# Eight turns of an attention and gated-layer kernel in one written order, one copy moved to ScalarE, and W2's last results re-ordered

## The chip, the cores and the metric

One Trainium2 chip, one of its cores. The metric is the device time of one execution in microseconds (us). The kernel before took 838.37 us, the median of three runs (838.03 to 839.97).

## What is computed

Float64 weights and float32 activations come in; the output is float32. 3072 tokens of width 512 go through three layers:

```python
# 1. chunked attention, 8 heads of 64, queries in chunks of 32, 56 keys + 8 memory keys each
a = softmax(q_c @ k_full.T / 8);  x = a @ v_full
# 2. 512 -> 1024 -> 512
h = x @ w_in;  e = exp(h - max(h));  solu = h * e / (sum(e) + 1e-9)
ln = (solu - mean) / sqrt(var + 1e-6) * g_ln;  x2 = ln @ w_out
# 3. 512 -> 2048 -> 512
g = x2 @ w_in2;  out = max(0.01 * g, g) @ w_out2
```

All large products are split into a high and a low half (three 128x512 matmuls for one product of 128 rows), so that TensorE computes them at its full rate and the result keeps float32 accuracy. The float64 weights are decoded on the chip: an Abs on ScalarE, four VectorE operations on the raw words, then the halves.

## The kernel before, in words

**Tiles.** The tokens form 24 tiles of 128. A tile goes through these steps; the names are those of the profile.

- Attention of tile a: `s_scores` (32 small matmuls into `att`, L213, then a maximum on VectorE, L222 and L223), `s_exp` (eight exponentials on ScalarE, L230), `s_rs` (L237, L238), `s_pt` (four transposes into `tr`, L243, and a copy of the result to `pt` on VectorE, L248), `s_pv` (32 small matmuls, L264, and a scaling on VectorE, L270), `x_halves` (four transposes, L282, the high half on ScalarE, L286, the low half on VectorE, L288).
- First product: `h_steps`, 24 matmuls of 512 columns into `h` or into the tile `spare`, whose name in the profile is `x2p` (L299).
- The norm, `norm_steps`: maximum (VectorE, L315), exponential (ScalarE, L319), product and sum (VectorE, L321 to L328), square (ScalarE, L331), variance (VectorE, L333) and its power -0.5 (GpSimd, L335), and the final scaling, either on GpSimd (L338, L339, for the tiles in `ON_POOL`) or on VectorE (L341).
- Transposed halves of the result, `s_lt`: through TensorE in two groups of four transposes (L351, L353, L354), or, for the tiles in `BOUNCE`, through VectorE's transposes of 32x32 blocks and DRAM (`lt_steps`: L365, stored by L371, read back by L376, L389, L387).
- Second product, `s_o`: one of the four output chunks of a block of four tiles at a time, 24 matmuls of 512 columns into `x2p` (L401), then a copy on ScalarE and a store (`put_x2`, L409, L410). The program calls such a chunk a W2 result; there are 24.

**Stages.** (1) The startup decodes W1 and computes tiles 0 to 2 of the attention and the first product of tiles 0 and 1; its order is written out by hand in the string `STEPS`, one character for one step of a named stream. (2) Turns 0 to 7, a loop over `range(STEADY)`: turn i does the attention of tile i+2, the first product and the norm of tile i, the transposed halves of tile i-1, decodes some of the eight slices of W2 (`W2_AT`, `load_w2`: L114 to L129, L137, L138, and the low half on GpSimd, L140), and turn 7 also computes the first three W2 results (`O_AT`). This stage is issued in the order of the loop and each engine's order is then chosen by the compiler's planner. (3) Turns 8 to 24, the function `steady`, again in the written order on all engines (`manual_schedule`): one tile of attention, one tile's first product and one W2 result in each turn, five behind (`LAG`), and one slice of W3 decoded. Turn 24 has no tile left: it computes W2 result 19, the transposed halves of tile 23 and the last piece of W3. (4) The last four W2 results, 20 to 23, run while the third layer's operands are prepared (`x_steps`, L690 to L709; `w3_steps`, L725). (5) The third layer, in a scheme of seven products of half-size blocks (L841 and below).

**Queues.** Nearly all transfers are issued on the queue of the SP engine, in the order of issue: the queries (`load_q`), the keys (`kbd`) and values (`vbd`) of the next tile, the raw slices of W2 and W3 (`raw`). Keys and values have one buffer each, so their loads wait for the matmuls that read the tile before. `x2s`, the tile of `put_x2`, has one buffer; ScalarE issues its store, and in turn 24 also the two stores of the last W3 pair (L508, L509) and, for tile 6, the four reads of L376.

Of the kernel before, what the change touches and what calls it, by code (L numbers as in the profile page):

```python
# [33 lines left out]
ON_POOL = range(6)  # L34

SPARE_PSUM = (1, 3, 5)
# [8 lines left out]
def tile_kernel(  # L45
# [99 lines left out]
    def decode(raw, dh, dl, pool, gain=None, sub=nc.gpsimd):  # L145
        for _ in decode_steps(raw, dh, dl, gain, pool, sub):
            pass
        return lows[-1]


# [48 lines left out]
    def load_tile(i):  # L199
        return *load_qk(i), load_kv(i, vbd, vw)  # L200

    def load_w2(kk):
        decode(
            load_raw(w2[kk * P : (kk + 1) * P, :], dec), w2h[:, kk], w2l[:, kk],
            dec, g_sb[:, kk : kk + 1],
        )

    def s_scores(i, q, k):
        sc = ps_att.tile([P, 8, 64], F32, name="att")
        for hp in range(4):  # L210
            for c in range(4):
                cs = slice(32 * c, 32 * c + 32)
                nc.tensor.matmul(  # L213
                    sc[cs, 2 * hp : 2 * hp + 2, :], q[:, hp, cs], k[:, :, hp, c, :],
                    start=True, stop=True,
                )
        if i % TPB == 0:
            nc.vector.memset(sc[0:32, :, 8:24], NEG)
# [5 lines left out]
        return sc, nms  # L224
# [15 lines left out]
    def pt_steps(p):  # L240
# [7 lines left out]
        nc.vector.tensor_copy(pt, ptp)  # L248
# [6 lines left out]

    def s_pt(p):
        return last(pt_steps(p))
# [17 lines left out]
    def s_pv(pt, v, rs):  # L275
        return last(pv_steps(pt, v, rs))

# [13 lines left out]
    def x_halves(x):  # L291
        return last(xt_steps(x))

# [10 lines left out]

    def s_h(x, h=None, early=False):
        if x is not None:
            if h is None:
                h = ps_h.tile([P, DFF], F32, name="h")
            for _ in h_steps(*x, h):
                pass  # L310
        return last(norm_steps(h, early))
# [32 lines left out]
    def s_lt(so, b, t, lh, ll):  # L344
        ts_ = slice(t * P, (t + 1) * P)
        if TB * b + t not in BOUNCE:
            for g in range(2):
                tp = ps_tr.tile([P, 4, P], F32, name="tr")
                for kk in range(4):
                    f = (4 * g + kk) * P  # L350
                    nc.tensor.transpose(tp[:, kk], so[:, f : f + P], ident)  # L351
                cs = slice(4 * g, 4 * g + 4)
                nc.scalar.activation(lh[:, cs, ts_], tp, AF.Copy)  # L353
                nc.vector.tensor_tensor(  # L354
                    out=ll[:, cs, ts_], in0=tp, in1=lh[:, cs, ts_].bitcast(F32), op=ALU.subtract
                )
            return
        for _ in lt_steps(so, b, t, lh, ll, nc.scalar):
            pass

    def lt_steps(so, b, t, lh, ll, eng):
# [7 lines left out]
        yield  # L369
# [5 lines left out]
        for q in range(4):  # L375
            eng.dma_start(  # L376
# [17 lines left out]
    def s_o(b, ec, lh, ll, part, s=None):  # L394
        if part == 0:
# [3 lines left out]
        for kk in range(4 * part, 4 * part + 4):  # L399
# [5 lines left out]
        if part == 1 and s != 0:  # L405
            put_x2(b, ec, lp.tile([P, BT], F32, name="x2s", bufs=1) if s is None else s)
# [5 lines left out]
    def att_steps(i, ld):  # L412
# [5 lines left out]
        pt = s_pt(p)  # L418
        yield
        x = s_pv(pt, ld[2], rs)  # L420
# [15 lines left out]
    startup = ExitStack()  # L436
    startup.enter_context(
# [48 lines left out]
    startup.close()  # L486
    del xs[:2]
    ld = load_tile(3)
    sst.close()
    lp = sh.enter_context(tc.tile_pool(name="lp", bufs=2, reuse_waits="tile"))  # L490
    lb = {}
    w3m = []
    so = None

    def store_w3(f, m, eng=nc.sync):
# [12 lines left out]
        eng.dma_start(out=w3f[f // 2, :, 2:4], in_=a)  # L508
        eng.dma_start(out=w3f[f // 2, :, 4:7], in_=s)  # L509
# [7 lines left out]
    def leftover(o):  # L517

        o.so = next(o.norm)
        put_x2(*o.x2, lp.tile([P, BT], F32, name="x2s", bufs=1))  # L520
# [6 lines left out]
    def steady(i, o):  # L527
# [4 lines left out]
        def w2(j):  # L532
            s_o(j // TB, j % TB, *lb[j // TB], 0)
            s_o(j // TB, j % TB, *lb[j // TB], 1, 0)
            u.x2 = j // TB, j % TB
# [5 lines left out]
        else:  # L541
            w2(i - LAG)
            store_w3(f - 1, lows[-1], nc.scalar)
# [3 lines left out]
        if i - 1 in BOUNCE:  # L547
            u.lt = lt_steps(o.so, *to, nc.sync)
            next(u.lt)
# [35 lines left out]
        w2(i - LAG)  # L585
        for _ in w3d:
            pass
        next(u.norm)
# [11 lines left out]
    for i in range(STEADY):  # L600
        a = i + 2
        b, t = divmod(i, TB)
        if t == 0:
            lhl = lp.tile([P, 2, KF, BT], F32R, name="lhl")
            lb[b] = (lhl[:, 0], lhl[:, 1])
        att = a > 2
        if att:
            p, rs = s_exp(*s_scores(a, ld[0], ld[1]))
            s_rs(rs)
        if i == max(SPARE_PSUM) + 1:  # L610
            sx2.close()
            ps_x2 = sx2.enter_context(tc.tile_pool(name="ps_x2b", bufs=2, space=PSUM, side="right", reuse_waits="tile"))
        if i < 2:
            nso = s_h(None, hs[i], True)
        else:
# [544 lines left out]
```

## Time and profile before

| | |
|---|---|
| median of three runs | 838.37 us |
| the profiled execution: its own time | 840.38 us |
| the profiled execution: its span, first to last instruction | 838.4 us |
| mean granted TensorE clock | 0.998 of full |
| startup, to the last matmul of tiles 0 and 1 | 0 to 38.6 us |
| turns 0 to 7, to the start of turn 8 | about 38.6 to 130.7 us |
| turns 8 to 24 | about 130.7 to 353 us |
| the last W2 results | about 353 to 377.3 us |
| third layer | 377.3 to 838.4 us |

The profile gives for each engine the time in which it was busy; a matmul's end is modelled, so a row of back-to-back matmuls of 0.39 us each that start every 0.23 us counts as busy throughout. "PEld" is TensorE's loading of weights, "granted clock" the share of TensorE's full clock, of which there are two levels (1.2 and 2.4 GHz); a stretch with a share between has some of each.

### The profile page before, as it was taken

Reading aid. Unit: us, or ns where it says so; the run is one execution under the profiler, and the core shown is the slowest. Engines: PE = TensorE matmul, PEld = TensorE weight load, DVE = VectorE, ACT = ScalarE, POOL = GpSimd, SP = SyncE. Lnnn points to the kernel's source line nnn. Section 1 sums busy time; section 2 is a strip of 40 time slices with the busy share of each in tenths; the row PEclk is TensorE's granted clock in tenths of the full one; section 3 lists DMA queues with packets and bytes.
Section 4 is the critical chain, followed back from the end, with each engine's and each line's share of the span. In section 5 each row is a group of like instructions: output and inputs, shape, how many; then the busy total and the mean of one; then the engine's idle time right before and its main releaser. Section 6 shows DMA issues by size and latency. Waiting matters only on the chain.

```text
span 838.4 us, 13730 instructions
## 1 busy us (share of the span) xinstructions
PE 816.3 (97%) x5014; PEld 666.2 (79%) x5014; DVE 649.7 (77%) x1145; ACT 472.9 (56%) x1067; POOL 54.9 (7%) x63
## 2 busy tenths in 40 slices
PE   6889999999999999999999999999999999999998
PEld 5566778888888888778888888888888888888886
DVE  8989865888888888698888855675699687768663
ACT  5478844555546553457655656677658344544541
POOL 3333300000000000000000000000000000010001
PEclk9999999999999999999999999999999999999999
DMA  9555554888879785833898964586696375546542
GB/s 337 192 165 188 164 189 129 270 261 258 263 252 272 257 247 187 295 127 107 289 339 325 342 233 197 198 325 258 247 382 225 121 255 194 196 164 220 192 147 101
DMA packets 69891, 190.96 MB, mean 228 GB/s; under 512 B 8000, under 2 KB 32064, under 8 KB 65856
## 3 DMA queue, kind: packets, MB, share of 16 engines
q1 hardware_dynamic: 65360, 182.61, 63.4%
q10 hardware_dynamic: 4464, 7.47, 2.4%
q8 instruction: 40, 0.66, 0.3%
q14 instruction: 27, 0.22, 0.1%
HBM read 129.24 MB, written 60.82 MB: 227 GB/s over the span
## 4 chain that ended last, share of the span: by engine, by line
PE 86%; DVE 6%; ACT 4%; POOL 1%; DMA 1%; issue 1%; ACTq 0%; DVEq 0%; POOLq 0%
PE C L841 27%; PE B L841 16%; PE x2p L401 13%; PE A L841 12%; PE h L299 12%; PE att L264 2%; PE att L213 2%; PE tr L282 1%; PE tr L243 1%; ACT p L230 1%; POOL w2l L140 1%; PE x2p L299 1%; DMA kbd<-in_kw 1%; DVE hnm L315 1%; ACT e L331 1%
## 5 line engine op out<-in xcount | busy, mean ns | idle before, releaser
L401 PE MATMUL x2p<-lhl,w2h 128*128 128x512 f32 x384 | 121.2, 396 | 2.0 <-ACT xP L409 1.6
L841 PE MATMUL C<-xP,L 128*128 128x512 f32 x384 | 95.2, 389 | 0.0
L401 PEld LDWEIGHTS x2p<-lhl,w2h 128*128 128x128 f32 x384 | 70.6, 188 | 19.9 <-issue 3.0
L841 PEld LDWEIGHTS C<-xP,L 128*128 128x128 f32 x384 | 72.1, 188 | 15.0
L401 PE MATMUL x2p<-lhl,w2l 128*128 128x512 f32 x192 | 75.1, 391 | 0.0
L299 PE MATMUL h<-w1h,xh 128*128 128x512 f32 x168 | 68.9, 410 | 0.0
L299 PE MATMUL h<-w1h,xl 128*128 128x512 f32 x168 | 66.7, 397 | 1.6 <-DVE xl L288 1.6
L841 PE MATMUL C<-h,L 128*128 128x512 f32 x192 | 66.9, 389 | 0.0
L299 PE MATMUL h<-w1l,xh 128*128 128x512 f32 x168 | 66.4, 395 | 0.0
L949 DVE TENSOR_TENSOR ring<-ring,h 128x512 fp32r<-128x512 f32 x96 | 61.8, 685 | 3.3 <-ACT h L948 2.7
L230 ACT ACTIVATE p<-att,nms 128x64 f32<-128x64 f32 x192 | 57.4, 335 | 6.5 <-DVE nms L223 6.1
L948 ACT ACTIVATE h<-ring 128x512 fp32r<-128x512 f32 x72 | 39.8, 621 | 31.8 <-DMA ring<-gd 19.3
L864 ACT ACTIVATE g<-g 128x512 f32<-128x512 f32 x72 | 45.2, 627 | 21.9 <-DVE g L883 19.0
L319 ACT ACTIVATE e<-h,hnm 128x1024 f32<-128x1024 f32 x21 | 23.5, 1121 | 57.1 <-DVE hnm L315 57.1
L841 PE MATMUL B<-xP,L 128*128 128x512 f32 x192 | 48.9, 390 | 0.0
L948 ACT ACTIVATE h<-t2k 128x512 fp32r<-128x512 f32 x48 | 28.6, 628 | 31.5 <-DVE t2k L941 17.1
L883 DVE TENSOR_TENSOR g<-B,u 128x512 f32<-128x512 f32 x23 | 15.9, 690 | 36.0 <-PE B L841 35.9
L230 ACT ACTIVATION_READ_ACCUMULATOR p<-att,nms 128x1 f32 x192 | 42.7, 222 | 0.0
L401 PEld LDWEIGHTS x2p<-lhl,w2l 128*128 128x128 f32 x192 | 36.1, 188 | 7.6
L841 PEld LDWEIGHTS B<-xP,L 128*128 128x128 f32 x192 | 36.0, 188 | 7.7 <-DVE g L893 0.3
L841 PEld LDWEIGHTS C<-h,L 128*128 128x128 f32 x192 | 36.0, 188 | 7.5
L299 PEld LDWEIGHTS h<-w1h,xl 128*128 128x128 f32 x168 | 31.8, 190 | 9.4 <-DVE xl L288 2.7
(187 smaller groups left out, 1913.0 us busy)
## 6 DMA issues: line engine op xcount, KB each, us to landing
ring<-gd SPq DMA_DIRECT2D x48, 768.0 KB, 4.0
gd<-g SPq DMA_DIRECT2D x24, 1024.0 KB, 4.9
raw<-in_w SPq DMA_DIRECT2D x32, 512.0 KB, 5.8
L<-w3f SPq DMA_DIRECT2D x14, 896.0 KB, 5.7
kbd<-in_kw SPq DMA_DIRECT2D x46, 256.0 KB, 4.4
vbd<-in_vw SPq DMA_DIRECT2D x46, 256.0 KB, 3.8
lnd<-sl SPq DMA_DIRECT2D x16, 512.0 KB, 4.5
xtq<-in_w SPq DMA_DIRECT2D x16, 512.0 KB, 6.3
```

The costliest lines, as they stand in the source:

```text
L140: sub.tensor_tensor(out=dl, in0=m, in1=dh.bitcast(F32), op=ALU.subtract)
L213: nc.tensor.matmul(sc[cs, 2 * hp : 2 * hp + 2, :], q[:, hp, cs], k[:, :, hp, c, :], start=True, stop=True,)
L230: nc.scalar.activation(p[:, h // 2, :, h % 2], sc[:, h], AF.Exp, bias=nms[:, h : h + 1], scale=SCALE, accum_out=rs[:, h : h + 1],)
L264: nc.tensor.matmul(xp[cs, 2 * hp : 2 * hp + 2, :], pt[:, hp, cs], v[:, :, hp, c, :], start=True, stop=True,)
L299: nc.tensor.matmul(h[:, hf * 512 : hf * 512 + 512], a[:, kk], b, start=kk == 0 and j == 0, stop=kk == KD - 1 and j == 2,)
L319: nc.scalar.activation(e, h, AF.Exp, bias=nm, accum_out=rs)
L401: nc.tensor.matmul(ps, a[:, kk, es], r[:, kk], start=(kk == 0 and n == 0), stop=(kk == KF - 1 and n == 2),)
L841: nc.tensor.matmul(acc, w[i], x[j], start=first and n == 0, stop=last and n == 2, skip_group_check=True)
L864: nc.scalar.activation(u.g[:, i], u.g[:, i] if src is None else src, AF.Prelu, alpha=0.01)
L883: tt(out=o.g[:, 1], in0=o.acc["B"], in1=o.u2, op=ALU.add)
L948: nc.scalar.activation(h[:, i], src[n_], AF.Copy)
L949: tt(out=l[:, i], in0=src[n_], in1=h[:, i].bitcast(F32), op=ALU.subtract)
```

## The change

- **One order for turns 0 to 7.** The planner's stage goes. The work of turns 0 to 7 becomes streams of steps: `a` to `h` for the attention of tiles 3 to 10, `0` to `7` for the norms, `i` to `p` for the slices of W2, `A` to `F` for the first products of tiles 2 to 7, `G` to `R` for the transposed halves of tiles 0 to 5 (two groups each), `S` for those of tile 6, `T`, `U`, `V` for W2 results 0 to 2. The last nine steps of `STEPS` join them as `w`, `x`, `y` and `z`. The string `TURNS` of 303 characters gives the order, the same for all five engines.
- **The copy of the transposed probabilities** of tiles 3 to 10 is made by ScalarE (`PT_DVE` is empty).
- **The final scaling of tile 7** goes to GpSimd (`ON_POOL`), from VectorE; tile 6 keeps VectorE.
- **Tile 6's reads from DRAM** (L376) are issued by SP, and no more by ScalarE.
- **Turn 23**: one step of the norm is called between the steps of the decode. **Turn 24**: W2 result 19 is cut into two halves of 12 matmuls, with the transposed halves of tile 23 between them; the norm's last step and `put_x2` come ahead of the last W3 pair's VectorE work and stores.
- **Last W2 results**: five instead of seven steps of `x_steps` come ahead of result 20 and its copy, three more follow that copy.

```diff
-    "zb4155243AAbA5bc4AB766c456B7ABc6B55776B67cABc7ABABc"
+    "zb4155243AAbA5bc4AB766c456B7ABc6B55776B67c"
-W2_AT = {1: (0,), 2: (1,), 3: (2, 3), 6: (4, 5), 7: (6, 7)}
+TURNS = (
+    "iaaiwxxaxi0zy0yizaaa0ybajbiAj0AAAi1bA0A1abAbbj0a1aca1cbGGABcBbbBb2GBjcBbkdk2dcHBjB1j2BcckH"
+    "CC1HcCdle3d23cdcld2CCeckCCIe2J3JC4IdfIk34DJDDdkeeldd3DefDDKfdlLDD3eg4KKLmM4lMLmfefE55EmEME"
+    "lmfEEnNme5n54EgnEmTNNTngeUUTUU45fh6oOe6PTnUoTO56nOFoo66FFppopPpPT6fFFFSFUggQpoUTgpFTUSgRQ7"
+    "QTfV7RhhUVfRV7VhV7VVVgfg7S7hgSgVh"
+)
+PT_DVE = ()
-O_AT = {7: (0, 1, 2)}
-ON_POOL = range(6)
+ON_POOL = (0, 1, 2, 3, 4, 5, 7)
...
-        nc.vector.tensor_copy(pt, ptp)
+        if vector:
+            nc.vector.tensor_copy(pt, ptp)
+        else:
+            nc.scalar.activation(pt, ptp, AF.Copy)
...
         else:
-            w2(i - LAG)
-            store_w3(f - 1, lows[-1], nc.scalar)
+            w2(i - LAG, range(4))
         if o.norm:
             leftover(o)
...
         if i == NTILE:
             s_lt(o.so, *to)
-            put_x2(*u.x2, lp.tile([P, BT], F32, name="x2s", bufs=1))
+            w2(i - LAG, range(4, KF))
+            last = store_w3(f - 1, lows[-1], None)
+            put_x2(*u.x2, x2_tile())
+            for dst, src in last:
+                nc.scalar.dma_start(out=dst, in_=src)
             return u
...
         w2(i - LAG)
+        if i == NTILE - 1:
+            next(w3d)
+            next(u.norm)
         for _ in w3d:
             pass
-        next(u.norm)
+        if i < NTILE - 1:
+            next(u.norm)
...
+    ld = [*load_qk(3)]
+    raws = [load_w2raw(0), load_w2raw(1)]
+    load_kv(3, vbd, vw)
...
+    for c in TURNS:
+        next(streams[c])
...
-    for _ in range(7):
+    for _ in range(5):
         next(xs0)
-    for n, (j, s) in enumerate(zip(range(NTILE + 1 - LAG, NTILE), (x2t[:, 0], x2t[:, 1], None, 0))):
-        s_o(j // TB, j % TB, *lb[j // TB], 0)
-        s_o(j // TB, j % TB, *lb[j // TB], 1, s)
+    for n, j in enumerate(range(NTILE + 1 - LAG, NTILE)):
+        s_o(j % TB, *lb[j // TB])
+        if n < 3:
+            put_x2(j // TB, j % TB, x2t[:, n] if n < 2 else x2_tile())
         if n == 0:
+            next(xs0)
+            next(xs0)
             next(xs0)
```

In the new streams the keys and the query of tile a+1 are loaded right behind the scores of tile a, its values behind the second product of tile a, and the raw slice kk+2 of W2 behind the fourth step of slice kk.

## Rows read from the trace of the kernel before

**Rows 1.** The page, part 1: busy time of each engine.
```profile
PE 816.3 (97%) x5014; PEld 666.2 (79%) x5014; DVE 649.7 (77%) x1145; ACT 472.9 (56%) x1067; POOL 54.9 (7%) x63
```

**Rows 2.** Busy time by stretch: from:to, length, engines, granted clock, DMA.
```profile
core 0: us, PE busy (x) PEld busy (x) DVE busy (x) ACT busy (x) POOL busy (x), PEclk, DMA share, GB/s
33.30:130.70 97.40, 89.13 (x837) 67.23 (x828) 77.50 (x170) 64.58 (x195) 25.82 (x24) 0.98 0.50 166
...
44.00:47.00 3.00, 3.00 (x10) 2.35 (x10) 2.42 (x7) 3.00 (x8) 0.31 (x1) 0.61 0.49 165
144.58:158.47 13.89, 13.89 (x122) 11.45 (x121) 11.15 (x25) 7.73 (x25) 0.55 (x1) 1.00 0.88 263
...
340.72:377.29 36.57, 34.52 (x155) 27.89 (x154) 28.75 (x37) 17.92 (x25) 0.66 (x1) 1.00 0.56 209
```

**Rows 3.** The chain that ended last, in order of time: start, length, what.
```profile
144.58 5.46 PE h L299 x24
...
329.21 5.44 PE x2p L401 x24
```

**Rows 4.** Timeline from 339 us: start, length, engine, line, [idle before, releaser].
```profile
339.93 1.03 PE L351 MATMUL tr<-ident,so 128*128 128x128 f32 x8
...
340.72 0.71 PE L401 MATMUL x2p<-lhl,w2h 128*128 128x512 f32 x2
...
348.14 0.66 POOL L335 TENSOR_TENSOR rstd<-ve,mhalf 128x1 f32<-128x1 f32 x1 [10.84 <-DVE ve L333]
...
349.56 0.81 DVE L341 TENSOR_SCALAR so<-so,nmu,rstd 128x1024 f32<-128x1024 f32 x1
...
354.05 0.40 PE L401 MATMUL x2p<-lhl,w2l 128*128 128x512 f32 x1
...
361.30 1.06 ACT L690 ACTIVATE xP<-xt 128x1024 fp32r<-128x1024 f32 x1 [2.87 <-DVE xt L695]
...
365.61 0.58 ACT L409 ACTIVATE xP<-x2p 128x512 f32<-128x512 f32 x1
...
366.24 0.74 PE L401 MATMUL x2p<-lhl,w2h 128*128 128x512 f32 x2 [1.58 <-ACT xP L409]
```

**Rows 5.** Timeline of the startup's end.
```profile
33.98 2.97 POOL L140 TENSOR_TENSOR w1l<-m,w1h 128x512 fp32r<-128x512 f32 x2 [1.29 <-ACT w1h L138]
...
39.11 1.21 DVE L315 TENSOR_REDUCE hnm<-x2p 128x1 f32<-128x1024 f32 x1
...
42.60 0.33 PE L243 MATMUL tr<-ident,p 128*128 128x128 f32 x1 [2.97 <-ACT p L230]
```

**Rows 6.** Groups between 34 and 130.7 us: busy us, mean ns, idle before.
```profile
L140 POOL TENSOR_TENSOR w2l<-m,w2h 128x512 fp32r<-128x512 f32 x8 | 10.6, 1330 | 23.8 <-ACT w2h L138 23.8
...
L353 ACT ACTIVATE lhl<-tr 128x512 fp32r<-128x512 f32 x12 | 7.2, 612 | 2.5 <-PE tr L351 2.4
L339 POOL TENSOR_SCALAR so<-so,rstd,nmu 128x1024 f32<-128x1024 f32 x6 | 7.2, 1203 | 2.9 <-DVE nmu L338 1.8 <-DVE nms L223 0.7 <-DVE hrs L321 0.4
...
L248 DVE COPY pt<-tr 128x512 f32<-128x512 f32 x7 | 4.7, 671 | 1.5 <-PE tr L243 1.5
...
L341 DVE TENSOR_SCALAR so<-so,nmu,rstd 128x1024 f32<-128x1024 f32 x2 | 1.6, 812 | 1.2 <-POOL rstd L335 1.2
...
L338 DVE TENSOR_SCALAR nmu<-nmu,rstd 128x1 f32<-128x1 f32 x6 | 1.3, 212 | 2.0 <-POOL rstd L335 1.9
```

**Rows 7.** The page, part 6: DMA issues, KB each, us to landing.
```profile
raw<-in_w SPq DMA_DIRECT2D x32, 512.0 KB, 5.8
```

**Rows 8.** Timeline near 56 and 44 us: a VectorE operation beside GpSimd, and alone.
```profile
44.44 0.70 DVE L124 SCALAR_TENSOR_TENSOR m<-raw,m 128x512 uint32<-128x512 uint32 x1
...
55.61 1.20 POOL L339 TENSOR_SCALAR so<-so,rstd,nmu 128x1024 f32<-128x1024 f32 x1 [0.43 <-DVE nmu L338]
...
55.95 1.40 DVE L124 SCALAR_TENSOR_TENSOR m<-raw,m 128x512 uint32<-128x512 uint32 x1
```

More of the change, by code (lines that the diff above doesn't have):

```diff
@@ L398, in s_o @@
         es = slice(ec * P, (ec + 1) * P)
-        for kk in range(4 * part, 4 * part + 4):
+        for kk in part:
             for n, (a, r) in enumerate(((w2h, lh), (w2h, ll), (w2l, lh))):
@@ L404, in s_o, with x2_tile @@
                 )
-        if part == 1 and s != 0:
-            put_x2(b, ec, lp.tile([P, BT], F32, name="x2s", bufs=1) if s is None else s)
+            yield
+    def s_o(ec, lh, ll, part=range(KF)):
+        for _ in o_steps(ec, lh, ll, part):
+            pass
+    def x2_tile():
+        return lp.tile([P, BT], F32, name="x2s", bufs=1)
     def put_x2(b, ec, s, eng=nc.scalar):
@@ L507, in store_w3 @@
         tt(out=s[:, 2], in0=b[:, 1], in1=s[:, 1], op=ALU.subtract)
-        eng.dma_start(out=w3f[f // 2, :, 2:4], in_=a)
-        eng.dma_start(out=w3f[f // 2, :, 4:7], in_=s)
+        pair = (w3f[f // 2, :, 2:4], a), (w3f[f // 2, :, 4:7], s)
+        if eng is None:
+            return pair
+        for dst, src in pair:
+            eng.dma_start(out=dst, in_=src)
     def load_w3raw(f):
@@ new lines, in tile_kernel, with turn_att @@
+    load_kv(3, vbd, vw)
+    halves, sos = {}, {}
+    hs = dict(enumerate(hs))
+    turn = Turn()
+    def turn_att(a):
+        sc = score_steps(a, *ld)
+        next(sc)
+        ld[:] = load_qk(a + 1)
+        yield
+        sc = next(sc)
+        yield
+        p, rs = s_exp(*sc)
+        yield
+        s_rs(rs)
+        yield
+        pt = pt_steps(p, a in PT_DVE)
+        next(pt)
+        yield
+        pt = next(pt)
+        if a == STEADY + 2:
+            turn.pt, turn.rs = pt, rs
+            yield
+            return
+        yield
+        x = pv_steps(pt, vbd, rs)
+        next(x)
+        load_kv(a + 1, vbd, vw)
+        yield
+        x = next(x)
+        yield
+        xt = xt_steps(x)
+        next(xt)
+        yield
+        halves[a] = next(xt)
+        yield
+        next(xt)
+        yield
@@ new lines, in turn_h, with turn_norm, turn_lt @@
+    def turn_h(i):
+        h = spare if i % 2 and i < STEADY - 2 else ps_h.tile([P, DFF], F32, name="h")
+        hs[i] = h
+        yield from h_steps(*(halves.pop(i) if i in halves else xs[i]), h)
+    def turn_norm(i):
+        for sos[i] in norm_steps(hs[i], i in ON_POOL):
+            yield
+    def turn_lt(i, *g):
+        nonlocal lp
+        if not lb:
+            sst.close()
+            lp = sh.enter_context(tc.tile_pool(name="lp", bufs=2, reuse_waits="tile"))
+            new_lhl(0)
+            new_lhl(1)
+        yield from (lt_group if g else lt_steps)(sos[i], i // TB, i % TB, *lb[i // TB], *g)
@@ L646, in tile_kernel @@
+    for n in range(3):
+        streams["TUV"[n]] = turn_o(n)
+    for c in TURNS:
+        next(streams[c])
+    turn.so = sos[STEADY - 1]
+    xs[:] = [halves[STEADY], halves[STEADY + 1]]
     for i in range(STEADY, NTILE + 1):
```

180 lines of the change are left out of this document (70 added, 110 removed).

## The prediction

> **What bounds the kernel now.** I read the page's busy times first. TensorE is busy for 97% of the span, VectorE for 77%, ScalarE for 56% [rows 1]; TensorE is the engine to shorten, and by that row only some 22 us of the whole kernel are free. The busy time by stretch shows where. From 144.58 to 158.47 us, one turn of the steady stage, TensorE never pauses at the full clock, and the turn lasts 13.89 us; from 33.30 us, where TensorE reaches the first step that the change re-orders, to 130.70 us it is busy for 89.13 of 97.40 us, and a part of it, 44 to 47 us, at a granted share of 0.61, so for the most part at 1.2 GHz [rows 2]. I take 130.70 us as the end because turn 9 begins at 144.58 us in the chain of waits [rows 3] and a turn is 13.89 us long: what comes before 130.70 us is turns 0 to 7 and all that they leave behind.
>
> The busy row still flatters this stretch, so I count the work instead. 24 matmuls of the first product take 5.46 us from start to start, 24 of a W2 result 5.44 us [rows 3]. The steady turn is one of each and one tile of attention, so attention costs TensorE 13.89 - 5.46 - 5.44 = 2.99 us. Eight transposes take 340.72 - 339.93 = 0.79 us from the first to the next matmul [rows 4]. In the stretch TensorE has: the last 18 matmuls of tiles 0 and 1 (18/24 x 5.46 = 4.10), four transposes of tile 2 (0.40), the attention of tiles 3 to 9 (7 x 2.99 = 20.93) and half of it for tile 10 (1.50), the first product of tiles 2 to 7 (6 x 5.46 = 32.76), the transposes of tiles 0 to 5 (6 x 0.79 = 4.74), three W2 results (16.32). The sum is 80.75 us. The stretch takes 97.40 us, so **16.65 us are waiting, half clock or gaps**.
>
> The page "Trainium Kernel Development and Optimization" of the Trainium skill, section Performance Expectations, says that matmul busy time tells badly how near a kernel is to its limit, because matmuls are pipelined, and that the busy share of the weight loads tells it better. The trace agrees: weight loads are busy for 67.23 of 97.40 us here and for 11.45 of 13.89 us in a steady turn [rows 2], and at the steady share the stretch would last 67.23 x 13.89 / 11.45 = 81.6 us. Going by the busy row instead, no more than 97.40 - 89.13 = 8.27 us could be won, and with the other terms below the sum would be about 831 us.
>
> What TensorE waits for is not one engine. VectorE is busy for 77.50 us of the stretch, ScalarE for 64.58 [rows 2], and all three hand to each other in a fixed order. A typical wait is that of 42.60 us: the transposes of the probabilities stood 2.97 us behind ScalarE's exponentials, which stood behind VectorE's two maxima of tiles 0 and 1, the second at 39.11 us [rows 5].
>
> **The change, part by part.**
>
> *Loads on the engines.* The eight copies of the transposed probabilities leave VectorE: 8 x 0.671 = 5.4 us. On ScalarE the trace has no such copy; the nearest row is its copy of the same shape out of the same kind of tile, 0.612 us [rows 6]. Between 0 (where ScalarE is idle) and 8 x 0.671 I take 4.9 us. Tile 7's final scaling costs VectorE 0.81 us less and 0.21 more, GpSimd 1.20 more [rows 6]. VectorE then has 77.5 - 5.4 - 0.6 = 71.5 us of work, ScalarE 69.5, GpSimd 27, TensorE 80.75. TensorE has the most, by 9 us; in the steady turn VectorE's share is 11.15 / 13.89 = 0.80 [rows 2] and TensorE doesn't wait, here it would be 71.5 / 82 = 0.87. So TensorE can set the pace, if the order is good.
>
> *The order.* I summed the work of each engine along the string of steps, with the durations above. TensorE's sum and VectorE's stay within 2 us of each other over the first third, then TensorE's runs ahead by 5 to 7 us, ScalarE's stays beside VectorE's. Each matmul step has its producer at least a few steps ahead in the producer's own queue: the scores of a tile come before the second product of the tile before it, the first W2 results are spread between the steps that decode the W2 slices they read. I found one wait that can't go: the last step of tile 0's first product reads the low half of the last W1 slice, which GpSimd finishes at 33.98 + 2.97 = 36.95 us [rows 5]. TensorE, with 32 scores and two steps first (1.0 + 1.4 us), is at it at 35.7 us and its second matmul has to stand about **1.0 us**. The scores of tile 3 now come before that and the exponentials before the maxima, so the 2.97 us behind ScalarE go, and with no long pause the half clock at 44 to 47 us goes too.
>
> For the other waits I have no row; the bounds are 0, as in the steady turn, and 8.3 us, half the present excess. An order in which each engine has 10 to 15% to spare is nearer to the steady turn: I take **2.0 us**. The stretch then lasts 80.75 + 1.0 + 2.0 = 83.75 us: **13.65 us less**. What hides the rest is TensorE's own work; were the order worse than I read it, VectorE is late next.
>
> *Moved transfers.* The raw slices of W2 are issued two slices ahead; the Abs that reads one stands, by TensorE's sum, 7 us behind its issue at the tightest (slice 3), 10 to 15 us else, and a load lands after 5.8 us [rows 7]. Behind a late one on ScalarE stand the exponentials. The key and query loads are issued right behind the scores, seven us before the next ones. Tile 6's four reads leave ScalarE's queue and stand on SP's, where they wait for their own store; behind them are the values of tile 10 and the keys of tile 11, needed only in turn 8. All at nothing; the cover is TensorE's work between, and without it a slice would cost what it is late by.
>
> *Turn 23.* The step of the norm that is called between the decode's steps is ScalarE's square; what it is moved past is VectorE's. No engine's own order changes: 0 us, and below or above nothing only by the waits' bookkeeping.
>
> *Turn 24.* From 340.72 to 377.29 us TensorE has six W2 results and eight transposes, 6 x 5.44 + 0.79 = 33.4 us of 36.57 [rows 2]; 3.1 us are the most that the end can give. The norm's last step stood on VectorE behind four operations of the W3 pair and ran at 349.56 us; its power is done at 348.80 us [rows 4], so it can run 0.7 us earlier and end at 349.7. The first 12 matmuls of result 19 begin at about 346.2 us (340.72 + 5.44) and end at 348.9; TensorE waits 0.8 us, transposes to 350.5, ends result 19 at 353.2 and goes on to result 20 without the present gaps. Now result 20's third matmul starts at 354.05 us [rows 4], which at 0.227 a matmul is a start at 353.6. Gain 0.4; bounds 0 and 0.8.
>
> *Last W2 results.* Result 22 now waits 1.58 us, for the copy of result 20 at 365.61 us, which stands on ScalarE behind four splits [rows 4]. Two of these go behind it: it can start when the split of 361.30 us ends, 362.4 us, and is done at 363.0, ahead of result 21's end (364.6 us). Gain 1.5; bounds 0 and 1.58. The splits that come later are then on ScalarE behind a short copy, and the third layer reads them after 377 us. Together with turn 24 **1.9 us**.
>
> **Sum**: 13.65 + 1.9 = 15.5 us. The profiled execution's span is 838.4 us and its own time 840.38, 2.0 us around it and 2.0 above the median of 838.37; I take the difference off the median: **822.9 us**. The third layer runs with TensorE busy throughout, so nothing of it is given back there.
>
> **The rivals.**
>
> (a) *Half the excess stays.* The copies stand on ScalarE's queue behind the eight exponentials of the next tile, and second products wait for them. For it: ScalarE is to be 85% busy. Against it: VectorE's relief. 8.3 + 1.9 = 10.2 us less: 828.2 us.
>
> (b) *VectorE is slowed by GpSimd.* An operation of 0.70 us took 1.40 us beside GpSimd's scaling [rows 8]. If each of GpSimd's 8 low halves and 7 scalings stretches one by 0.70 us, VectorE has 71.5 + 10.5 = 82 us, begins about 2 us after TensorE, and the stretch ends with its tail behind it, at some 87 us: 10.4 + 1.9 us less, 826.1 us. The page "SBUF — State Buffer" of the Trainium skill, section "SBUF: two separate sides", has the rule: GpSimd and a VectorE operation with two SBUF inputs share a port pair, and the one that comes second stands until the first has ended. Rows 8 agree, and by that rule the move of tile 7's scaling speaks against the change. Against it: the mean of GpSimd's low halves, 1330 ns [rows 6], and VectorE's 77.50 us already hold such overlaps.
>
> (c) *Slower.* SP now has one written order, and a load that waits for its tile holds all behind it. If the raw slices of W2 land some 14 us after their place in the order instead of 5.8 [rows 7], ScalarE stands at each of six Abs, slices 2 to 7, with the exponentials behind it. At 3.5 us each that is 21 us against a gain of 15.5: 843.9 us. It decides from 2.6 us a slice.
>
> (d) *The order does nothing.* The planner's waits were true dependences and return elsewhere; only the end gains: 838.4 - 1.9 = 836.5 us.
>
> **How the numbers follow.** The forecast with its bounds (0 to 4 us of waits, 1 to 2.3 us at the end) gives 820.5 to 826 us and has a chance of 0.62; (a) has 0.17, (b) 0.12, (c) 0.04, (d) 0.05. The range is 820.5 to 829.0 us: forecast, (b) and most of (a). A measurement of this kernel can tell about 0.3%, 2.5 us, from no change; (d) is within that. Faster 0.62 + 0.17 + 0.12 = 0.91, same 0.05, slower 0.04.
>
> **What would show it.** Right: the third layer's first matmul some 15 us earlier; no wait over 1 us on TensorE between 38 and 115 us but the one at 36 us; a granted clock of 1.0 from 38 us on; weight loads busy for about 80% of the stretch; VectorE's work there 71 to 73 us; result 22 without its wait. Wrong: TensorE waiting again and again for `pt` or `p` from ScalarE (a), VectorE busy for 80 us or more (b), Abs waiting for `raw` (c), a stretch of 95 us or more (d).

## The result and the profile after

The changed kernel takes **825.41 us** (median of 5 runs, 824.44 to 825.91); the kernel before took 839.19 us beside it (5 runs, 838.03 to 839.97). The ratio is 0.9837, with a 95% interval of 0.9827 to 0.9848: 13.8 us faster. The profiled execution has a span of 823.8 us instead of 838.4, and its own time is 825.91.

The page of the changed kernel, part 1 (busy time of each engine) and the first line of part 4 (the chain that ended last, by engine):

```profile
PE 812.1 (99%) x5014; PEld 669.2 (81%) x5014; DVE 646.6 (78%) x1137; ACT 476.1 (58%) x1075; POOL 56.3 (7%) x64
...
PE 96%; DVE 2%; DMA 1%; issue 0%; SPq 0%; POOL 0%; DVEq 0%; ACT 0%; POOLq 0%
```

TensorE's share rose from 97% to 99% [rows 1], a step that looks small for 14 us. The busy row held back again: 816.3 us of "busy" became 812.1 with the same 5014 matmuls, so at least 4 us of the old figure were half clock and gaps that the modelled ends covered.

I measure the turns from the start of tile 2's product of probabilities and values (`s_pv`) to the start of tile 8's first product, and the end from tile 23's first product to the third layer's first matmul; the first products' starts are taken from the chain of waits. Before, tile 8's first product is in pieces, so I take tile 9's (144.58 us [rows 3]) less one steady turn of 13.88 us. Each such figure comes from one profiled execution of its kernel. The turns went from 98.20 us (32.50 to 130.70) to 85.38 (32.76 to 118.14), the end from 42.64 us to 40.45; 12.8 + 2.2 = 15.0 us. The third layer took 461.1 us in both. The remaining 0.4 us are the startup (32.76 against 32.50) and small differences in the steady turns.

Busy time by stretch after the change (from:to, length, engines, granted clock, DMA), the turns and one steady turn:

```profile
core 0: us, PE busy (x) PEld busy (x) DVE busy (x) ACT busy (x) POOL busy (x), PEclk, DMA share, GB/s
33.56:118.14 84.58, 82.87 (x839) 67.57 (x830) 73.37 (x162) 69.36 (x217) 25.33 (x24) 1.00 0.58 191
...
132.02:145.90 13.88, 13.88 (x122) 11.45 (x121) 11.50 (x25) 7.71 (x25) 0.55 (x1) 1.00 0.78 244
```

Against [rows 2] the weight loads have the same work (67.57 and 67.23 us) in 13 us less, the clock is whole, VectorE lost 4.1 us and ScalarE gained 4.8. The steady turn is as before.

All waits of TensorE between 33 and 119 us after the change (us in total, times, longest):

```profile
PE att L204 <- DMA kbd<-in_kw: 1.4, 1, 1.4
PE h L288 <- POOL w1l L143: 0.3, 1, 0.3
```

Before, the same question gave five waits, 8.2 us together, with that of [rows 5] the longest:

```profile
PE tr L243 <- ACT p L230: 4.1, 3, 3.0
PE tr L351 <- POOL so L339: 2.0, 3, 0.8
PE x2p L299 <- ACT xh L286: 1.1, 1, 1.1
PE tr L351 <- DVE pt L248: 0.8, 1, 0.8
PE tr L282 <- DVE nmu L328: 0.2, 1, 0.2
```

None of them is left. What remains is the low half of W1's last slice, which I had forecast, and a key load, which I had not.

The timeline after the change (start, length, engine, line, idle before and releaser): one operation of VectorE in the startup's end, which the last section comes back to, then the end of the W2 results, with the norm of tile 23, the transposes of its result, and then all that is left of the W2 results as one piece of the chain of waits in the second fence.

```profile
35.88 1.18 DVE L215 TENSOR_SCALAR nms<-nms 128x8 f32<-128x8 f32 x1
...
336.34 0.81 DVE L322 TENSOR_SCALAR so<-so,nmu,rstd 128x1024 f32<-128x1024 f32 x1 [0.73 <-POOL rstd L316]
...
337.30 1.06 PE L330 MATMUL tr<-ident,so 128*128 128x128 f32 x8 [0.55 <-DVE so L322]
...
350.01 0.58 ACT L398 ACTIVATE xP<-x2p 128x512 f32<-128x512 f32 x1
```

```profile
338.36 24.51 PE x2p L384 x108
```

The 1.58 us wait of result 22 [rows 4] is gone: the copy of result 20 is done at 350.59 us, and result 22 begins near 351.8. The 108 matmuls follow each other without a pause.

### The profile page after: what moved, and what is told of

Same layout as the page of the kernel before. It is cut to its first block, busy times and chain, and to the rows that moved or that the text cites. A ratio compares the mean times of both kernels' runs of the same rounds, so it can differ in the third digit from the quotient of the medians.

```text
span 823.8 us, 13739 instructions
## 1 busy us (share of the span) xinstructions
PE 812.1 (99%) x5014; PEld 669.2 (81%) x5014; DVE 646.6 (78%) x1137; ACT 476.1 (58%) x1075; POOL 56.3 (7%) x64
## 4 chain that ended last, share of the span: by engine, by line
PE 96%; DVE 2%; DMA 1%; issue 0%; SPq 0%; POOL 0%; DVEq 0%; ACT 0%; POOLq 0%
PE C L889 28%; PE B L889 16%; PE x2p L384 15%; PE h L288 14%; PE A L889 12%; PE att L259 3%; PE att L204 2%; PE x2p L288 2%; PE tr L274 1%; PE tr L238 1%; PE tr L330 1%; PE x2p L459 1%; DMA kbd<-in_kw 1%; DVE m L127 0%; DVE m L132 0%
## 5 line engine op out<-in xcount | busy, mean ns | idle before, releaser
L1131 POOL TENSOR_TENSOR u<-u,s 128x512 f32<-128x512 f32 x6 | 7.7, 1300 | 465.4 <-DVE u L1124 465.4
```

## The experiments

Twelve more kernels ran. "Turns" and "end" are the two stretches above, from the profiled execution of each; the time is the median, with the ratio to the kernel before on the same chip and its interval.

| kernel | time, us | ratio | turns | end | span |
|---|---|---|---|---|---|
| before | 839.2 | 1 | 98.20 | 42.64 | 838.4 |
| changed | 825.41 | 0.9837 (0.9827 to 0.9848) | 85.38 | 40.45 | 823.8 |
| turn 23 undone | 824.93 | 0.9830 (0.9817 to 0.9843) | 84.51 | 40.49 | 823.1 |
| end undone | 825.84 | 0.9837 (0.9824 to 0.9850) | 84.52 | 41.83 | 823.9 |
| copies back on VectorE | 827.40 | 0.9859 (0.9845 to 0.9872) | 86.67 | 40.45 | 825.3 |
| four copies back | 824.68 | 0.9830 (0.9816 to 0.9843) | 84.35 | 40.45 | 822.1 |
| no scaling on GpSimd | 824.89 | 0.9833 (0.9818 to 0.9847) | 85.21 | 40.48 | 824.4 |
| key load first | 824.85 | 0.9827 (0.9814 to 0.9840) | 84.49 | 40.48 | 823.5 |
| W1's last low half on VectorE | 824.24 | 0.9825 (0.9811 to 0.9838) | 83.83 | 40.48 | 822.1 |
| products in blocks, last place | 844.49 | 1.0074 (1.0051 to 1.0097) | 104.72 | 40.46 | 842.2 |
| products in blocks, middle | 832.79 | 0.9919 (0.9895 to 0.9944) | 93.00 | 40.48 | 831.6 |
| before + copies on ScalarE | 838.00 | 0.9989 (0.9980 to 0.9997) | 96.66 | 41.66 | 834.7 |
| before + new end | 837.65 | 0.9983 (0.9974 to 0.9992) | 98.21 | 40.46 | 835.6 |
| before in loop order | 970.88 | 1.1564 (1.1546 to 1.1581) | about 229 | 41.41 | 969.6 |

### Which part carries the gain

**The copies on ScalarE alone, under the planner.** The kernel before, with one edit:

```diff
-        nc.vector.tensor_copy(pt, ptp)
+        nc.scalar.activation(pt, ptp, AF.Copy) if late else nc.vector.tensor_copy(pt, ptp)
...
-            pt = s_pt(p)
+            pt = s_pt(p, True)
...
```

> The kernel before with the copies of the transposed probabilities of tiles 3 to 10 on ScalarE, the planner's order otherwise. Theory 1 (the order carries the gain, the copy is worth 2 us in it): 834 to 840 us. Rival (VectorE's 5.4 us are what the planner's turns lack): 833 us or less.

Measured: 838.00 us, 0.1% faster. Busy time from 33.30 to 130.70 us in that kernel:

```profile
33.30:130.70 97.40, 90.41 (x836) 69.03 (x835) 72.87 (x163) 69.34 (x217) 25.48 (x24) 0.98 0.53 173
```

VectorE fell from 77.50 us [rows 2] to 72.87, ScalarE rose to 69.34: these are the loads of the changed kernel. TensorE still waited 4.0 us for ScalarE's exponentials, and 1.5 us were won in the turns of this execution, which is the fastest of its twelve. The planner also chose another order (tile 7's first product comes in pieces of 6 and 18 matmuls instead of 5 and 19). The loads alone were not what bound the turns.

**The order without the copies.** The changed kernel with

```diff
-PT_DVE = ()
+PT_DVE = range(3, 11)
```

> The changed kernel with the eight copies of the transposed probabilities back on VectorE, in the same places of the order. VectorE's work in turns 0 to 7 rises from 73.4 to about 78.7 us, ScalarE's falls to 64.5. Theory 1 (the order carries the gain, the copy only makes room): 825 to 827.5 us, 1 to 4 above 823.8. Rival (the copy's move is what brings it): the 5.4 us of VectorE come back whole, 829 us or more. Third (VectorE has room enough): 823.8, within 0.5.

Measured: 827.40 us, and turns of 86.67 us; all four of its times (827.18 to 828.02) lie above the five of the changed kernel (824.44 to 825.91). So the order (with tile 7's scaling) took 98.20 - 86.67 = 11.5 us out of the turns, and the copies another 2.2 us against the 84.51 us of the kernel with turn 23 undone, which has the same order of turns. TensorE's waits from 33 to 131 us in that kernel show where:

```profile
PE att L259 <- DVE pt L244: 0.9, 1, 0.9
PE h L288 <- DVE so L306: 0.6, 1, 0.6
PE tr L330 <- POOL so L320: 0.6, 1, 0.6
```

They stand at 62, 43 and 52 us, and two of them wait for VectorE directly. The first and the third are new; the second is 0.2 us with turn 23 undone.

**Four of the eight copies.** The same switch with only tiles 7 to 10:

```diff
-PT_DVE = ()
+PT_DVE = (7, 8, 9, 10)
```

> Edit: the changed kernel, but the copies of the transposed probabilities of tiles 7 to 10 are made on VectorE (those of tiles 3 to 6 stay on ScalarE). With all eight on VectorE the stretch was 2.2 us longer. Theory 1: a copy costs time on VectorE only where its queue is filled and TensorE has little other work to put in between; the new waits of all eight on VectorE stood at 43 to 62 us, with tiles 4 to 6, and after 65 us none was seen. So these four cost nothing: stretch 84.5 to 84.9 us, time 824.9 to 825.7 us. Rival: each copy on VectorE costs its share, 2.2/8 us, or it is the later four that carry it: stretch 85.6 to 86.7 us, time 826 to 827.4 us.

Measured: 824.68 us, turns 84.35 us: the four late copies cost nothing, so the 2.2 us belong to the four early ones, or need all eight.

**No scaling on GpSimd.** VectorE makes all final scalings of turns 0 to 7:

```diff
-ON_POOL = (0, 1, 2, 3, 4, 5, 7)
+ON_POOL = ()
```

> The changed kernel with all final scalings on VectorE (0.81 us each there instead of a product of 0.21 and GpSimd's 1.20). VectorE's own work rises by 7 x 0.6 = 4.2 us. Theory 1 (VectorE is next to TensorE, each microsecond put on it early in the turns comes back in part): 825 to 828 us. Rival (GpSimd's scalings stretch VectorE's operations by 0.4 to 0.7 us each, so that VectorE gains as much as it gets): 823 to 824.5 us, with VectorE busy for no more than 74 us in the turns.

Measured: 824.89 us, turns 85.21 us; neither theory's numbers. Busy time over the turns, first of this kernel, then of the one with all copies on VectorE, then of the changed kernel with turn 23 undone (which has the order of the changed one):

```profile
33.53:118.74 85.21, 84.16 (x860) 68.11 (x860) 77.36 (x162) 69.43 (x217) 17.97 (x19) 1.00 0.58 193
```

```profile
32.34:119.01 86.67, 84.08 (x860) 68.17 (x860) 77.48 (x170) 66.47 (x210) 25.22 (x25) 1.00 0.55 186
```

```profile
32.48:116.99 84.51, 83.82 (x860) 68.26 (x860) 74.29 (x163) 69.57 (x217) 25.50 (x25) 1.00 0.59 194
```

The group of one of VectorE's two-input operations (busy us, mean ns) over the same stretch reads alike, word for word, without the scalings on GpSimd and with turn 23 undone, where they are there:

```profile
L132 DVE SCALAR_TENSOR_TENSOR m<-raw,m 128x512 uint32<-128x512 uint32 x10 | 8.6, 859 | 0.1
```

Without the scalings on GpSimd VectorE works 77.36 us, with the copies 77.48, both some 3.1 us over 74.29. The same load costs 0.7 us of the turns in the one kernel, with no difference in the time that the intervals can tell, and 2.2 us in the other. **VectorE's load alone does not decide.** That the place in the chain of hand-overs does is argued and not shown: a copy stands between two of TensorE's own groups and a final scaling is wanted only some turns later, but the four late copies stand between such groups too and cost nothing. What the three kernels do show is that work put on VectorE early in the turns, where TensorE comes to wait for it at 43 to 62 us, has a price, and the same copies later have none.

Nor did GpSimd's leaving the scalings quicken VectorE. With turn 23 undone six operations of VectorE between 31 and 117 us (lines L127, L132 and L215) are 0.3 to 1.1 us longer than others of their line; each of them runs beside one of GpSimd's low halves, none beside a scaling. Without the scalings there are again six, all beside low halves.

**The end alone, on the kernel before**, its core:

```diff
-            w2(i - LAG)
-            store_w3(f - 1, lows[-1], nc.scalar)
+            w2(i - LAG, (0,))
...
+            w2(i - LAG, (1,))
+            pair = store_w3(f - 1, lows[-1], None)
...
-    for _ in range(7):
+    for _ in range(5):
...
```

> The kernel before with the new order of turn 24 and of the last W2 results alone. Theory 1: what that part is worth is the wait of result 22 and two gaps, 1 to 2.2 us (in the kernel with this part undone the wait was 0.8 us, in the kernel before 1.6): span 836.2 to 837.4 us, and from the last first product to the end 501.5 us as in the changed kernel, instead of 502.9 to 503.8. Rival (the end's gain needs the new turns): 838.4 us.

Measured: 837.65 us, end 40.46 us against 42.64. By the trace 2.2 us, by the median 1.5 us.

**The end undone in the changed kernel**, the same edits the other way, its core:

```diff
-            w2(i - LAG, range(4))
+            w2(i - LAG)
+            store_w3(f - 1, lows[-1], nc.scalar)
...
-    for _ in range(5):
+    for _ in range(7):
...
```

> The changed kernel with turn 24 and the last W2 results in their old order. Theory 1 (the order of turns 0 to 7 brings most, the end 2 us by itself): span 825.8 us, 2.0 above the changed kernel's 823.8, with the wait of result 22 back at 1.5 us. Rival (what the end wins is given back or hidden): 823.8 us, within 0.5.

Measured: 825.84 us, end 41.83 us. TensorE's waits from 319 us on in that kernel:

```profile
PE x2p L384 <- ACT xP L398: 0.8, 1, 0.8
PE x2p L384 <- ACT lhl L333: 0.3, 1, 0.3
PE x2p L384 <- DVE lhl L335: 0.2, 1, 0.2
```

They are the three that the kernel before shows in its end, but result 22's is 0.8 us instead of 1.58 [rows 4]. Ahead of ScalarE's splits stands the copy of result 19 into `x2s`, which waits until the store before it has left that one buffer: 1.26 us in the kernel before, 0.47 here.

```profile
354.68 0.60 ACT L409 ACTIVATE x2s<-x2p 128x512 f32<-128x512 f32 x1 [1.26 <-DMA x2d<-x2s]
```

```profile
340.25 0.60 ACT L398 ACTIVATE x2s<-x2p 128x512 f32<-128x512 f32 x1 [0.47 <-DMA x2d<-x2s]
```

Two more kernels with the old end bear this out: with the copies alone this copy waits 0.30 us and result 22 0.6, in the loop order (below) it waits for no store and result 22 0.4. So the old end takes 42.64, 41.83, 41.66 and 41.41 us in these four, by how early that store has landed, and the new one 40.45 to 40.49 in ten: it is worth 0.9 to 2.2 us in the traces. By the medians it is 0.4 us here, by the ratios to the kernel before nothing (0.9837 in both), and 1.5 on the kernel before; with so small a part only the traces tell it.

**Turn 23 undone**:

```diff
-        if i == NTILE - 1:
-            next(w3d)
-            next(u.norm)
         for _ in w3d:
             pass
-        if i < NTILE - 1:
-            next(u.norm)
+        next(u.norm)
```

> The changed kernel with turn 23's calls in the old sequence. Theory 1 (no engine's own order changes by that edit): the changed kernel's time, span 823.8 us within 1; what it differs by shows how far two executions of one order lie apart, above all whether the wait for tile 4's keys is there again. Rival (the edit pulls the norm of tile 23 ahead): its step of the variance 1.4 us later than now and the end longer by up to 1.4 us.

Measured: 824.93 us, end 40.49 us against 40.45. Around turn 23 each engine's instructions come in the same order with and without the edit. This kernel is therefore a second execution of the changed one, and its turns, 84.51 us, show what the changed kernel does without the 1.43 us wait for the key load.

### What in the order does it

**The loops' order, written.** Before, a planner sorted the work of turns 0 to 7. Here the kernel before keeps its code and gives up the planner: all engines run the steps in the order of the loops.

```diff
-    startup.close()
...
-    order_ctx = ExitStack()
-    order_ctx.enter_context(tc.manual_schedule(engines=ENGS))
+    order_ctx = startup
```

> The kernel before, with turns 0 to 7 fixed in the order in which its loop is written, on all engines, without the planner. Theory 1 (it is the interleaving of this order that fills TensorE): slower than before, 850 to 865 us, TensorE waiting in each turn for the probabilities, the copy and the norm. Rival (any fixed order does it, the planner's choices cost the time): 826 to 830 us.

Measured: 970.88 us, far beyond both. Its larger TensorE waits over the whole span, one of ScalarE's, and two rows of the page's part 2 (slices of 24 us; tenths of busy time, then of the granted clock):

```profile
PE tr L351 <- DVE pt L248: 39.6, 6, 7.2
PE tr L243 <- ACT p L230: 39.3, 11, 10.3
PE tr L282 <- DVE x L270: 15.3, 8, 10.3
```

One of ScalarE's waits over the whole span, which was 8.4 us in all before:

```profile
ACT m L114 <- DMA raw<-in_w: 40.7, 9, 9.2
```

The page's rows:

```profile
PE   6646526624899999999999999999999999999998
...
PEclk9876557767899999999999999999999999999999
```

Each tile's attention is one chain from engine to engine, and with little between its links TensorE stands through most of it, then runs the next piece at a lower clock. A second cause is in the same edit: in the loop's order a raw slice of W2 is loaded only right ahead of its Abs, so ScalarE stands for it, and four such loads are 22 us of the chain of waits. A fixed order is worth nothing by being fixed: this one is 16% slower than the planner, the one of the change 1.6% faster. How much of the 970.88 us the loads, and how much each engine's order, brought is open; so this kernel alone does not show that the interleaving does it.

**The first products in one block.** In the string of the change the eight steps of a first product stand between other steps. Gathered at the place of the last (first piece of the string shown; all other steps keep their order):

```diff
-    "iaaiwxxaxi0zy0yizaaa0ybajbiAj0AAAi1bA0A1abAbbj0a1aca1cbGGABcBbbBb2GBjcBbkdk2dcHBjB1j2BcckH"
+    "iaaiwxxaxi0zy0yizaaa0ybajbij0i1b01abbbj0a1aca1cbGGAAAAAAAAcbbb2Gjcbkdk2dcHj1j2BBBBBBBBcckH"
```

> Edit: the changed kernel, but in the fixed order the eight steps of each of the first products of tiles 2 to 7 (three matmuls each, 24 of 0.228 us or 5.46 us in a row) stand together at the place of the last of them, as the planner had left them; all other steps keep their order. Theory 1: the gain of the order comes from first products cut in pieces of 0.7 us that lie in TensorE's queue between the small groups of the attention, each while the other engines prepare the next one. With the pieces gathered, each small group up to the block waits with nothing to fill it, and what depends on the attention after the block comes up to 5.5 us later: of the 11.5 us that order alone brought, half or more is lost. Time 831 to 837 us, the stretch from the second product of tile 2 to the first of tile 8 90 to 97 us against 84.5, waits of 1 us and more on VectorE and ScalarE at TensorE. Rival: what counts is which group comes in which order and how early copies and scalings are issued, not the cutting; the other engines keep enough ahead: 825 to 827 us, 84.5 to 86.5.

Measured: 844.49 us, turns 104.72 us, longer than before the change and beyond the first theory's range. Busy time over the turns and TensorE's larger waits in them:

```profile
31.45:136.17 104.72, 90.11 (x860) 72.19 (x860) 74.04 (x163) 69.56 (x217) 25.42 (x25) 0.95 0.45 155
```

```profile
PE tr L330 <- DVE lhl L335: 4.9, 2, 3.6
PE tr L238 <- ACT p L225: 3.7, 4, 2.9
PE tr L330 <- ACT pt L246: 2.4, 1, 2.4
PE tr L330 <- POOL rstd L316: 1.2, 1, 1.2
```

**The same with the block at the place of the fifth step**, so that four steps come earlier and three later:

```diff
-    "iaaiwxxaxi0zy0yizaaa0ybajbiAj0AAAi1bA0A1abAbbj0a1aca1cbGGABcBbbBb2GBjcBbkdk2dcHBjB1j2BcckH"
+    "iaaiwxxaxi0zy0yizaaa0ybajbij0i1bAAAAAAAA01abbbj0a1aca1cbGGcbbb2GjcBBBBBBBBbkdk2dcHj1j2cckH"
```

> Edit: as the kernel with the first products of tiles 2 to 7 in one block each, but the block stands at the place of the fifth of the eight steps, not the last, so that four steps come earlier and three later than in the fixed order. With the block at the last place the stretch was 104.7 us against 84.5, 20 us longer. Theory 1: what costs is the block as such; TensorE has nothing to put between the small groups, whose producers need about as long as before, and each group behind the block is late by up to 5 us for the others. Then the place matters little: stretch 99 to 106 us, time 839 to 846 us, four or more waits of 1 us and over on TensorE. Rival: what cost was only that seven steps were moved late, so that the normalizations behind them came late; at the middle place the loss is small: stretch 85 to 90 us, time 826 to 831 us, no wait over 1 us but one.

Measured: 832.79 us, turns 93.00 us, between the two theories. TensorE's larger waits:

```profile
PE att L204 <- ACT p L225: 1.9, 1, 1.9
PE tr L238 <- DVE lhl L335: 1.5, 1, 1.5
PE tr L274 <- DVE x L265: 1.2, 2, 0.7
PE x2p L384 <- DVE so L306: 1.0, 1, 1.0
```

Both theories hold a part: the block in the middle costs 93.00 - 84.5 = 8.5 us, and the late place another 11.7 us. In this order a first product in one block loses 8.5 us or more at either of the two places; other places were not tried.

It does not follow that the cutting is what the written order has over the planner's. The expectation takes the planner's first products for blocks, and they are not. Tile 5's, for one, comes in six pieces of 6, 2, 2, 6, 5 and 3 matmuls, with transposes of other tiles between them:

```profile
79.58 0.40 PE L299 MATMUL x2p<-w1h,xl 128*128 128x512 f32 x1
79.99 0.33 PE L243 MATMUL tr<-ident,p 128*128 128x128 f32 x1
...
81.09 0.40 PE L299 MATMUL x2p<-w1l,xh 128*128 128x512 f32 x1
81.33 0.27 PE L243 MATMUL tr<-ident,p 128*128 128x128 f32 x1
81.36 0.48 PE L299 MATMUL x2p<-w1h,xl 128*128 128x512 f32 x1
```

In the changed kernel the same product comes in three, of 9, 9 and 6 matmuls from 72.75, 75.72 and 78.66 us, and those of tiles 2 to 7 in two or three pieces of 3 to 21 matmuls; a step is three matmuls, but several often stand together. The new order cuts less finely than the planner's (tile 7's excepted, 2 pieces before and 3 after). What it has over it is shown by the waits alone, 8.2 us of them before and 2.1 us in the three largest with the copies still on VectorE; which property of the order removes them stays open.

### The two waits that are left

**The key load first.** The values of tile 3 are issued on SP ahead of tile 4's keys; here they come behind:

```diff
-    load_kv(3, vbd, vw)
...
+        if a == 3:
+            load_kv(3, vbd, vw)
```

> The changed kernel with the values of tile 3 loaded behind the keys of tile 4 instead of ahead of them. The wait of 1.43 us that is left in the turns is for the keys of tile 4, which were issued 1.1 us behind the values. Theory 1 (the queue's order makes that wait): the wait falls to about 0.4 and the span to 822.7 us. Rival (tile 2's first product waits for the norm of tile 0 at the same point anyway, or the keys land no earlier): 823.8 us, within 0.3.

Measured: 824.85 us, turns 84.49 us. That is as long as in the kernels that lack this edit and did not show the wait (84.51 and 84.52). The 1.43 us wait belonged to one execution, and the edit brings nothing that can be measured.

**W1's last low half on VectorE**, and one place earlier in the order:

```diff
-    "iaaiwxxaxi0zy0yizaaa0ybajbiAj0AAAi1bA0A1abAbbj0a1aca1cbGGABcBbbBb2GBjcBbkdk2dcHBjB1j2BcckH"
+    "iaawixxaxi0zy0yizaaa0ybajbiAj0AAAi1bA0A1abAbbj0a1aca1cbGGABcBbbBb2GBjcBbkdk2dcHBjB1j2BcckH"
...
             got[f"w{n}"], w1h[:, hf, kk], w1l[:, hf, kk], None, sraw,
+            nc.vector if n == 7 else nc.gpsimd,
```

> Edit: the changed kernel, but the last low half of W1 is made on VectorE (one two-input operation of 128x512) instead of GpSimd, and stands one place earlier in the order, ahead of the first bit operations of W2's slice 0. Theory 1: the first product of tile 0's successor waits some 0.3 to 0.8 us in all for that low half, which GpSimd makes third in a row at 1.5 us each, ending at 37.0 us; VectorE can begin it once ScalarE's high half is there (35.3 us) behind the maximum (ends 35.8) and the scale, takes 0.7 to 0.8 us, and ends near 36.8. Gain at that wait 0.2 to 0.5 us, no other wait grows by more than 0.2; span 0.2 to 0.5 us less than the 823.1 to 823.8 of the kernels with this order, the time not to be told from 825.4 us. Rival: VectorE's 0.8 us more at this place delay tile 3's softmax and tile 0's normalization by as much, and scores or the normalized tile 0 come late instead: stretch longer by 0.3 to 1 us.

Measured: 824.24 us (824.01 to 825.09), turns 83.83 us, the lowest of all. Its timeline from 35 us:

```profile
35.80 0.17 DVE L215 TENSOR_SCALAR nms<-nms 128x8 f32<-128x8 f32 x1
35.88 0.68 DVE L143 TENSOR_TENSOR w1l<-m,w1h 128x512 fp32r<-128x512 f32 x1
...
36.62 0.50 PE L288 MATMUL h<-w1l,xh 128*128 128x512 f32 x1
```

The low half is made by 36.56 us and the last step's second matmul begins at 36.62, without a wait. The turns are 0.7 us shorter than 84.51, a little more than the 0.2 to 0.5 expected. The gain over the changed kernel, 1.2 us by the medians, is smaller than what can be told apart: the intervals of the two ratios overlap.

## Why the prediction was right, point by point

The forecast was 822.9 us with a range of 820.5 to 829.0, and 825.41 us lies in it. Of the 15.5 us, 14.6 show in the spans.

- **The work of the turns.** The count gave 80.75 us of TensorE work and 83.75 with waits, from the scores at 33.3 us on. Measured from there: 84.49 us in the changed kernel (33.65 to 118.14), 83.6 with turn 23 undone. So the waits added 2.9 us with turn 23 undone, where 3.0 were taken. The estimate from the weight loads, 81.6 us, was close, that from the busy row, 89 us, far off; so the rule of the Trainium skill, page "Trainium Kernel Development and Optimization", section Performance Expectations, held: weight loads are busy for 67.57 of 84.58 us, 80%, as predicted.
- **The order.** That the waits were made by the order and not by the work stood the test from both sides: the loads alone brought 1.5 us, the order alone 11.5. The two prices in it came out together and not one by one. The wait for W1's last low half was to be 1.0 us; it is 0.3 us in the changed kernel, and 0.5 us with turn 23 undone, where it falls on two steps. For all the rest 2.0 us were chosen between 0 and 8.3 without a row; 2.4 us are left with turn 23 undone. That was a good choice and no calculation, and here some luck is in the number.
- **The loads.** ScalarE has 69.36 us (69.5 predicted), a copy there 0.599 us (0.612 taken from [rows 6]). VectorE has 73.37 instead of 71.5, just above the 71 to 73 that were to show it. Of the difference 0.7 us is a misreading: the row has seven copies in the stretch [rows 6], and I moved eight. For the rest it is above all the scaling of the maxima (L215) that is longer, 4.2 us for eight operations where the kernel before has 2.3 for seven (L223): three of the eight take 0.84 to 1.28 us, the others 0.17.
- **The key loads, taken at nothing.** This is the step that failed in the profiled execution. I gave a load seven us before its scores. Tile 4's keys were issued at 35.75 us and TensorE was there at 40.8, so the cover was 5 us, and the load landed at 41.97. "No wait over 1 us but the one at 36 us" was therefore wrong for this execution. In eight other kernels with the load at the same place the scores of tile 4 began between 39.58 and 41.65 us with no wait for it.
- **The end.** 1.9 us predicted, 2.2 measured in the trace, 0.9 to 2.2 over the kernels with the old end. The wait of result 22 went as described; what I had not seen is that its 1.58 us hung on a store and is 0.4 to 0.8 us in the other three. In turn 24 TensorE waits 0.55 us for the normalized tile where 0.8 was worked out.
- **Turn 23**: 0 predicted, 0 measured.
- **From the trace to the time.** 0.8 of the 2.5 us between 822.9 and 825.41 is the median of before, 839.19 in these runs against the 838.37 that I started from. 0.9 is the gain missing from the span. The rest is that the profiled execution lies 1.2 us above the median before the change and 0.5 us after it.
- **The rivals.** (a) and (d) fell with the turns of 84.5 us, (c) with no Abs of W2 on the critical path; its mechanism is real, as the kernel in loop order shows. (b) fell with VectorE's 73.37 us where it needs 82: operations are stretched, but only some of GpSimd's low halves and none of its scalings meet one. What a stretched operation costs in time no run isolates.

What the prediction left open, and the runs leave open too, is *which* property of the order carries the gain. It spoke of producers a few steps ahead. The two kernels with blocks show that gathering each first product loses 8.5 us or more of the new order, but the planner's order had its first products cut as well. Of the 16.65 us of waiting, half clock and gaps that were counted, the five waits explain 8.2.

## What to carry to other kernels

Count TensorE's work from a stretch in which it never pauses, and set the sum against the stretch in question; the difference is the most that an order can win, whatever the busy row says. Lay the long independent product, in pieces, between the links of the dependent chain, where the other engines need time: in this order one block cost 8.5 to 20.2 us of the turns. Pieces alone do not make the order, the planner had them too. When moving work between engines, look where the bound engine will wait for it, and not at the load alone: some 3.1 us more work on VectorE cost 2.2 us of the turns as copies, 0.7 as final scalings, and the later half of the copies nothing.

## What was unexpected

- **A pause costs twice.** In the kernel in loop order the granted clock over the turns (33.30 to 261.58 us) is 0.69 of the full 2.4 GHz, and TensorE's own work becomes longer: 121.57 us of matmul time for the steps that took 89.13 [rows 2]. With the blocks at the last place it is 0.95. There TensorE was busy for 0.65 of the 2.12 us up to 83.12 us; then, after eight transposes and one matmul, seven start every 0.43 us (84.61 to 87.17 us, granted clock 0.50, which is 1.2 GHz), the next after 0.32, and from there on every 0.23 us. In the changed kernel it is 1.00 over the turns. The timeline of the kernel with the blocks at the last place:

```profile
83.12 1.27 PE L330 MATMUL tr<-ident,so 128*128 128x128 f32 x8 [1.22 <-POOL rstd L316]
...
84.61 0.63 PE L288 MATMUL x2p<-w1l,xh 128*128 128x512 f32 x1
85.04 0.63 PE L288 MATMUL x2p<-w1h,xl 128*128 128x512 f32 x1
...
86.75 0.63 PE L288 MATMUL x2p<-w1h,xh 128*128 128x512 f32 x1
87.17 0.48 PE L288 MATMUL x2p<-w1l,xh 128*128 128x512 f32 x1
87.49 0.40 PE L288 MATMUL x2p<-w1h,xl 128*128 128x512 f32 x1
```

- **A small operation can be stretched too.** VectorE's scaling of 128x8 elements at 35.88 us took 1.18 us in the changed kernel (first line of its timeline above) while GpSimd made a low half, ending at 37.06 us where the low half ended at 37.03. It took 0.17 us where that low half was VectorE's own (the fence of that experiment).
- **A load of 256 KB is not equally quick in each execution.** In the chain of waits of the changed kernel tile 4's keys are under way for 5.70 us from 36.27 us on. In the kernel with turn 23 undone they were issued 0.3 us earlier and the scores began at 40.59 us without a wait, so 4.6 us were enough. So a cover of about 5 us was enough in eight executions and not in one.
